# A two-block fp32 kernel on one core: a new order of loads, retention steps and weight rounding in its first segment

## The chip, the core and the metric

The kernel runs on one core of a Trainium2 chip. The metric is the device time of one execution in microseconds (us), as the median of several executions. Beside it stand single executions taken with the hardware profiler, whose span (first to last instruction) is about 1.8 us shorter than the time of the same execution. An execution is marked slow when it lies over 1.5% above the fastest of its kernel.

The engines are called by their short names where the profile does so: PE is the tensor engine's matmuls, DVE the vector engine, ACT the scalar engine, POOL GpSimd, SP the engine from which nearly all transfers are issued.

## The reference

A recurrent retention block, whose output feeds a SwiGLU feed-forward block, all in fp32 (batch 4, 8 heads, 768 positions, head size 64; model width 512, inner width 1536):

```python
for t in range(S):
    state = gamma * state + einsum('bhd,bhe->bhde', k[:, :, t], v[:, :, t])
    y[:, :, t] = scale * einsum('bhd,bhde->bhe', q[:, :, t], state)
x = y.transpose(0, 2, 1, 3).reshape(B * S, H * D)
g = x @ w_gate
out = (silu(g) * (x @ w_val)) @ w_out
```

## The kernel before

The kernel cuts the 3072 rows into four segments (`s` = 0 to 3) of six chunks of 128 rows. Retention of a chunk is three parts: `scores` (q times k, masked on DVE), `mix` (the output, copied by ACT into `xT`), `state` (update of the running state). All feed-forward products are done by a Strassen-like scheme with seven products for eight, so both factors need **sums**: S sums of the rows (`sums_x`), T sums of the weights (`sums_t`). The first segment goes through `up`, twelve units, one for each weight tile; as the weights come, they are rounded (three instructions on ACT, four on DVE, one addition on POOL: `convert_a`, `_b`, `_c`), summed and stored for the later segments, which use a second level of the scheme (`up2`). After each segment's up stage comes its down stage. The cuts of code below are shortened; `...` and comments stand for what is left out.

```python
def up(f):                       # one of 12 units of the first segment
    product(x, B11, a_up(0, 0)); copy(p1, x)
    if f: left[f - 1][0]()       # T4 product and both silus of the unit before
    sums_t(("up", f + 1, 0))     # DVE
    product(wb, T1, s1); copy(p5, wb)
    for p in at_block[f]: convert_b(p)          # DVE: half of a down tile, then the up tile
    for p in at_block[f][::-1]: convert_c(p)    # POOL: up tile, then the half
    product(x, T2, s2); copy(u2, x)
    product(wb, B22, s4)
    if f: left.pop(f - 1)[1]()   # DVE: both products with the gates
    tt(hT[:, f, 0], wb, u2, add)
    product(x, T3, s3); tt(hT[:, f, 1], x, p5, add)
    ...                          # convert_a of the next pieces (ACT), B21 product

# the start: all chunks loaded in order, a weight tile after chunks 2 and 4
retain(7); convert_a(u0); retain(3); convert_b(u0); convert_c(u0)
retain(3); sums_t(u0); retain(3); convert_a(u1); ...
for f in range(NF - 1): up(f)
...                              # T sums of the down tiles around the last up unit
```

In the first down stage, DVE also prepares the units of the second level between its other work: each is loaded from a store in DRAM, gets three sums, and is stored again. `step()` runs after every product (21 times).

```python
NU, RING = 21, 6                 # NU = 7 * NQ, NQ = 3
to_sum = list(range(RING - 1, NU, 2)) + list(range(RING - 2))   # 8 + 4 units
def step():
    k = count[0] = count[0] + 1
    retain((k > 2) + (4 < k < 13))            # retention of the next segment
    if count[1] * 20 < (k + 2) * len(to_sum): # one more unit's load
        load_unit(...); sums.extend(sums_u(n)); count[1] += 1
    while sums and count[2] * 20 < (k - 1) * 3 * len(to_sum):
        sums.pop(0)(); count[2] += 1          # the third sum also issues the store
```

## Time and profile before

| | before |
|---|---|
| median time | 743.3 us |
| span of the profiled run | 740.6 us |
| PE busy | 712.9 us (96%) |
| first product of S sums (T1 of unit 0) starts | 41.4 us |
| an up unit | 9.65 us |
| first down stage (end of the up stage to the next segment's second group of products) | 159.4 to 237.0 us |

### The profile page before, as it was taken

The numbers are of one execution on the slowest core, as the hardware profiler recorded it, in microseconds if no ns is written. First come the engines' busy times: TensorE is split into PE (matmuls) and PEld (weight loads), VectorE is DVE, ScalarE is ACT, GpSimd is POOL, SyncE is SP. The second block draws the span as 40 slices with busy tenths as digits, with TensorE's granted clock in tenths as the row PEclk, the third lists the DMA queues.
The fourth block names the chain that finished last, engine by engine and source line by source line (L and its number), as shares of the span: only waits on it lengthen the run. The fifth ranks groups of instructions, "written<-read, shape, count | busy, mean of one in ns | idle before, by whom it ended". The sixth has DMA issues, their size and how long they took to land.

```text
span 740.6 us, 11633 instructions
## 1 busy us (share of the span) xinstructions
PE 712.9 (96%) x4516; PEld 614.0 (83%) x4516; DVE 482.6 (65%) x829; ACT 241.8 (33%) x484; POOL 244.5 (33%) x152
## 2 busy tenths in 40 slices
PE   5789999999999999999999999999999999999997
PEld 5645555568888999997888999998888899999886
DVE  2899999997595787877454465758426356667420
ACT  2587777421211333321211324332121133233000
POOL 2533333423100547381210173454310053726000
PEclk9999999999999999999999999999999999999999
DMA  9968886458968667670643355660283055540010
GB/s 328 375 214 255 254 265 214 150 205 272 317 220 332 235 228 260 247 270 28 192 180 127 105 209 204 208 205 22 85 308 131 30 200 199 199 150 1 0 58 29
DMA packets 60823, 139.04 MB, mean 188 GB/s; under 512 B 4576, under 2 KB 27616, under 8 KB 60768
## 3 DMA queue, kind: packets, MB, share of 16 engines
q1 hardware_dynamic: 57312, 132.01, 52.2%
q10 hardware_dynamic: 3456, 6.29, 2.4%
q8 instruction: 35, 0.57, 0.3%
q14 instruction: 20, 0.16, 0.1%
HBM read 101.72 MB, written 36.57 MB: 187 GB/s over the span
## 4 chain that ended last, share of the span: by engine, by line
PE 82%; DVE 7%; issue 4%; POOL 2%; DMA 2%; ACT 2%; ACTq 0%; SPq 0%; DVEq 0%; POOLq 0%
PE bank L548 38%; PE bank L632 25%; PE bank L435 6%; PE bank L641 4%; PE bank L328 3%; PE bank L380 3%; PE bank L376 2%; POOL ring L265 2%; DVE ring L277 2%; PE bank L359 1%; DMA hT<-in_q_t_dram 1%; DMA hT<-in_k_t_dram 1%; DMA tab<-in_decays_dram 1%; DVE ring L252 1%; DVE xs L418 0%
## 5 line engine op out<-in xcount | busy, mean ns | idle before, releaser
L548 PE MATMUL bank<-loadp,ring 128*128 128x192 f32 x720 | 140.5, 327 | 2.8 <-ACT midp L513 2.8
L632 PE MATMUL bank<-wot,hsp 128*128 128x256 f32 x576 | 131.5, 383 | 0.0
L548 PEld LDWEIGHTS bank<-loadp,ring 128*128 128x128 f32 x720 | 120.5, 190 | 4.2 <-ACT midp L513 4.0
L632 PEld LDWEIGHTS bank<-wot,hsp 128*128 128x128 f32 x576 | 107.6, 190 | 16.3 <-issue 0.5
L513 DVE TENSOR_TENSOR iop<-bank,iop 128x384 f32<-128x384 f32 x144 | 79.7, 555 | 56.7 <-PE bank L548 53.6
L548 PE MATMUL bank<-xs,ring 128*128 128x192 f32 x432 | 87.8, 326 | 0.0
L513 POOL TENSOR_TENSOR iop<-hsp,midp 128x768 f32<-128x768 f32 x9 | 16.3, 1816 | 189.6 <-ACT hsp L513 149.4
L583 POOL TENSOR_TENSOR hT<-iop 128x768 f32<-128x768 f32 x36 | 66.5, 1848 | 35.8 <-DVE iop L513 35.8
L513 ACT COPY hsp<-bank 128x384 f32<-128x384 f32 x90 | 42.9, 479 | 99.5 <-PE bank L548 88.8
L548 PEld LDWEIGHTS bank<-xs,ring 128*128 128x128 f32 x432 | 73.1, 190 | 0.0
L435 PE MATMUL bank<-xs,ring 128*128 128x384 f32 x192 | 65.7, 497 | 2.8 <-DVE xs L418 2.8
L548 PE MATMUL bank<-xT,ring 128*128 128x192 f32 x324 | 66.2, 327 | 1.1 <-DVE iop L513 1.1
L632 PE MATMUL bank<-wot,hT 128*128 128x256 f32 x288 | 66.3, 383 | 0.0
L435 PEld LDWEIGHTS bank<-xs,ring 128*128 128x128 f32 x192 | 37.2, 194 | 29.5 <-DVE xs L418 3.4
L632 PEld LDWEIGHTS bank<-wot,hT 128*128 128x128 f32 x288 | 53.7, 190 | 8.5 <-issue 1.4
L548 PE MATMUL bank<-hsp,ring 128*128 128x192 f32 x288 | 56.8, 327 | 0.0
L513 DVE TENSOR_TENSOR midp<-bank,midp 128x384 f32<-128x384 f32 x72 | 40.0, 555 | 25.8 <-PE bank L548 24.3
L548 PEld LDWEIGHTS bank<-xT,ring 128*128 128x128 f32 x324 | 54.8, 190 | 2.3 <-DVE iop L513 2.2
L435 PE MATMUL bank<-xT,ring 128*128 128x384 f32 x144 | 51.0, 492 | 3.7 <-DVE hT L453 3.7
L548 PEld LDWEIGHTS bank<-hsp,ring 128*128 128x128 f32 x288 | 48.3, 190 | 0.5 <-ACT hsp L513 0.5
L435 PEld LDWEIGHTS bank<-xT,ring 128*128 128x128 f32 x144 | 26.5, 190 | 25.4 <-issue 9.0
L383 ACT COPY xT<-bank 128x512 f32<-128x512 f32 x24 | 14.1, 587 | 99.4 <-PE bank L380 96.6
(138 smaller groups left out, 983.4 us busy)
## 6 DMA issues: line engine op xcount, KB each, us to landing
ring<-unitt SPq DMA_DIRECT2D x50, 896.0 KB, 4.6
unitt<-ring SPq DMA_DIRECT2D x21, 896.0 KB, 4.6
unitb<-ring SPq DMA_DIRECT2D x12, 896.0 KB, 5.9
ring<-unitb SPq DMA_DIRECT2D x21, 512.0 KB, 5.7
out_dram<-iop ACTq DMA_DIRECT2D x24, 256.0 KB, 4.0
loadp<-in_w_val_dram SPq DMA_DIRECT2D x18, 256.0 KB, 5.8
loadp<-in_w_gate_dram SPq DMA_DIRECT2D x9, 512.0 KB, 6.4
midp<-in_w_out_dram SPq DMA_DIRECT2D x12, 256.0 KB, 3.1
```

The costliest lines, as they stand in the source:

```text
L265: nc.gpsimd.tensor_tensor(d.bitcast(I32), d.bitcast(I32), lo.bitcast(I32), op=ALU.add)
L277: sub(both, w[:, ds(B22, 2)], w[:, ds(B12, 2)], op=ALU.subtract)
L328: nc.tensor.matmul(sp[i][:, ts(n, P)], kt[r, n], qt[r, n], start=True, stop=True, skip_group_check=True)
L376: nc.tensor.matmul(y[r, ts(n, P)], prev[r, n], qd[r, n], start=(n == 0), stop=False, skip_group_check=True)
L380: nc.tensor.matmul(y[ds(D * i, D), ts(n, P)], vn[:, ts(2 * n + i, D)], a[i][:, n], start=(ci == 0 and n == 0), stop=True, skip_group_check ...
L383: nc.scalar.copy(xT[:, :, c // NCK % 2, ts(ci % L, P)], pairs(y))
L435: nc.tensor.matmul(o, w[:, slot, k], a[:, k], start=(start and k == 0), stop=(stop and k == KH - 1), skip_group_check=True)
L513: events.append((t, len(events), lambda: fn(*args, **kw)))
L548: nc.tensor.matmul(o[:, h], w[:, h, slot], rhs, start=(start and h == 0), stop=True, skip_group_check=True)
L583: by_block(9.5, 13.5, lambda r: pool(to[:, r], u2[:, r], p5[:, r], op=add))
L632: nc.tensor.matmul(o, a[:, k], wot[k][:, slot], start=(start and k == 0), stop=(k == FH - 1), skip_group_check=True)
L641: nc.tensor.matmul(o, a_dn(0, 0, u)[:, k], wot[k][:, B11], start=(k == 0), stop=(k == FH - 1), skip_group_check=True)
```

## The change

Its intent is to start the feed-forward products sooner. It replaces the loop of retention parts by a written order in which each letter is one part (s scores, m mix, t state, x S sums, a/b/c ACT's rounding, B/S DVE's, C POOL's, T T sums, U/D load of a tile), loads the last chunk ahead of the second weight tile, lets S sums read the retention output in PSUM, runs zero products at the very start, rounds the up tile ahead of the down half in each unit, moves the states of chunks 4 and 5 and the T sums of the down tiles into the first down unit, and starts the preparation of units later.

```diff
+    def sums_x(j): ...  # b(): the chunk's bank in PSUM instead of xT
-        tt(s1, a(1, 0), a(1, 1), op=ALU.add)
+        tt(s1, b(1, 0), a(1, 1), op=ALU.add)
...
+    do("""
+        s0 w6 s1 m0 m1 K0 t0 K1 s2 t1 g2 g3 Q2 s3 m2 x0 k2 q3 t2 s4 a0 b0 m3 k3 B0 t3 q4 c0
+        g4 s5 S0 g5 x1 m4 a1 q5 C0 U T0 b1 m5 x2 U D D
+    """)
...
+        beside[f, 1] = " ".join((each("BSC"), ...))     # up tile first
...
+            if s == 0:                                   # first down unit
+                sums_d(0); sum_h(1, 0)
+                second(0); do("t4")
+                sum_h(2, 0); sums_d(1)
+                second(1); do("t5")
+                sum_h(4, 0); sum_h(3, 0); sums_d(2)
...
-            retain((k > 2) + (4 < k < 13))
+            retain((k > 2) + (4 < k < 13) if s else (k > 5) + (7 < k < 18))
...
-            if count[1] < len(to_sum) and count[1] * 20 < (k + 2) * len(to_sum):
+            if count[1] < len(to_sum) and count[1] * 15 < (k - 5) * len(to_sum):
...
-            while sums and count[2] * 20 < (k - 1) * 3 * len(to_sum):
+            while sums and count[2] * 15 < (k - 6) * 3 * len(to_sum):
```

`second` is the B21 product, which used to stand between T3 and T4 of each row block; in the first two blocks of this stage T4 now follows T3 at once.

More of the change, by code (lines that the diff above doesn't have):

```diff
@@ L118, in places_of @@
         if n % 3 == 2:
-            return [ring[4 + i // 3][:, ts(i % 3, 512)] for i in range(4)]
+            return [ring[4 + i // 2][:, ts(i % 2, 512)] for i in range(4)]
         return [loadp[:, ts(4 * (n % 3) + i, 512)] for i in range(4)]
@@ L162, in load_unit, with sums_u @@
         units[n] = t
-    def sums_u(n):
+    def sums_u(n, engine=nc.vector):
         w = units[n]
-        sub = nc.vector.tensor_tensor
+        sub = engine.tensor_tensor
         def first():
@@ L207, in load_piece @@
             t = raw_places[kind].pop(0)
-            if kind == "down" or a > 1:
+            if kind == "down" or a:
                 raw_places[kind].append(t)
@@ L235, in words_of, with convert_a @@
         return d, r[:, :, 0], r[:, :, 1]
-    def convert_a(piece, *own):
+    def convert_a(piece, own, part=None):
         if piece in raw:
             d, lo, hi = words_of(piece)
-            nc.scalar.activation(d, hi.bitcast(F32), AF.Abs)
-            signs[piece] = []
-            for i, o in enumerate(own):
-                nc.scalar.copy(banks[o], hi[:, ts(i, 512)].bitcast(F32))
-                signs[piece].append(banks[o])
-            nc.scalar.activation(lo.bitcast(F32), lo, AF.Copy, scale=2.0 ** -51,
-                                 bias=2.0)
@@ L249, in convert_b @@
-    def convert_b(piece):
+            if part in (0, None):
+                nc.scalar.activation(d, hi.bitcast(F32), AF.Abs)
+            if part in (1, None):
+                signs[piece] = []
+                for i, o in enumerate(own):
+                    nc.scalar.copy(banks[o], hi[:, ts(i, 512)].bitcast(F32))
+                    signs[piece].append(banks[o])
+            if part in (2, None):
+                nc.scalar.activation(lo.bitcast(F32), lo, AF.Copy, scale=2.0 ** -51,
+                                     bias=2.0)
@@ new lines, in convert_b @@
+    def convert_b(piece, part=None):
+        if piece in raw:
+            d = words_of(piece)[0]
+            u = d.bitcast(U32)
+            if part in (0, None):
+                nc.vector.tensor_scalar(d, d, 122879.9921875, 2.0 ** -15, op0=ALU.min,
+                                        op1=ALU.max)
+                nc.vector.tensor_scalar(u, u, 3, None, op0=ALU.logical_shift_left)
+            if part in (1, None):
+                for i, t in enumerate(signs.pop(piece)):
+                    v = u[:, ts(i, 512)]
+                    nc.vector.scalar_tensor_tensor(v, t.bitcast(U32), 0x80000000, v,
+                                                   op0=ALU.bitwise_and,
+                                                   op1=ALU.bitwise_xor)
@@ L250, in convert_b, with convert_c @@
+    def convert_c(piece, halves=1):
         if piece in raw:
             d, lo, hi = words_of(piece)
-            nc.vector.tensor_scalar(d, d, 122879.9921875, 2.0 ** -15, op0=ALU.min,
-                                    op1=ALU.max)
-            u = d.bitcast(U32)
-            nc.vector.tensor_scalar(u, u, 3, None, op0=ALU.logical_shift_left)
-            for i, t in enumerate(signs.pop(piece)):
-                v = u[:, ts(i, 512)]
-                nc.vector.scalar_tensor_tensor(v, t.bitcast(U32), 0x80000000, v,
-                                               op0=ALU.bitwise_and,
-                                               op1=ALU.bitwise_xor)
@@ L262, in convert_c @@
-    def convert_c(piece):
-        if piece in raw:
-            d, lo, hi = words_of(piece)
-            nc.gpsimd.tensor_tensor(d.bitcast(I32), d.bitcast(I32), lo.bitcast(I32),
-                                    op=ALU.add)
+            n = d.shape[1] // halves
+            for i in reversed(range(halves)):
+                nc.gpsimd.tensor_tensor(d[:, ts(i, n)].bitcast(I32),
+                                        d[:, ts(i, n)].bitcast(I32),
+                                        lo[:, ts(i, n)].bitcast(I32), op=ALU.add)
@@ L267, in convert_c, with sums_t @@
             del raw[piece]
-        load_next(piece[0])
-    def sums_t(piece, engine=nc.vector):
+    def sums_t(piece, parts=range(3)):
         kind, a, h = piece
         w = span(piece)[0]
-        sub = engine.tensor_tensor
+        sub = nc.vector.tensor_tensor
         flat = w.rearrange("p a b -> p (a b)")
@@ L276, in sums_t @@
         both = flat[:, : 4 * n].rearrange("p (a b) -> p a b", b=2 * n)[:, :, :n]
-        sub(both, w[:, ds(B22, 2)], w[:, ds(B12, 2)], op=ALU.subtract)
-        sub(w[:, T2], w[:, B22], w[:, T1], op=ALU.subtract)
-        sub(w[:, T4], w[:, B21], w[:, T2], op=ALU.subtract)
+        for o, x, y in [((both, w[:, ds(B22, 2)], w[:, ds(B12, 2)])),
+                          ((w[:, T2], w[:, B22], w[:, T1])),
+                          ((w[:, T4], w[:, B21], w[:, T2]))][parts[0] : parts[-1] + 1]:
+            sub(o, x, y, op=ALU.subtract)
@@ L280, in sums_t, with scale @@
         if kind == "up":
             keep_wt(a)
-    at_block = [[("down", n // 2, n % 2) for n in range(2 * FH)
-                 if f == min(n, NF - 2)] +
-                [("up", f + 2, 0)] * (f + 2 < NF) for f in range(NF)]
+    pieces = [("up", f, 0) for f in range(NF)] + [
+        ("down", n % FH, 1 - n // FH) for n in range(2 * FH)]
+    sign_banks = {0: (0, 1), 1: (4, 5)}
+    def scale(what, engine):
+        return lambda n: what(cs[n], engine)
+    parts = {
+        "s": lambda n: scores(cs[n]), "m": lambda n: mix(cs[n]), "x": lambda n: sums_x(n),
+        "g": lambda n: decay(cs[n]), "t": lambda n: state(cs[n]), "w": lambda n: warm_up(n),
+        "k": lambda n: scale_k(cs[n]), "q": lambda n: scale_q(cs[n]),
+        "K": lambda n: scale_k(cs[n], nc.vector), "Q": lambda n: scale_q(cs[n], nc.vector),
+        "B": lambda n: convert_b(pieces[n], 0), "S": lambda n: convert_b(pieces[n], 1),
+        "C": lambda n: convert_c(pieces[n], 1 + (n == 0)), "T": lambda n: sums_t(pieces[n]),
+        "U": lambda n: load_next("up"), "D": lambda n: load_next("down"),
+        **{p: lambda n, i=i: convert_a(pieces[n], sign_banks.get(n, (6, 7)), i)
+           for i, p in enumerate("abc")}}
@@ new lines, in do @@
+    def do(order):
+        for o in order.split():
+            parts[o[0]](int(o[1:] or 0))
+    beside = {
+        (0, 0): "c1 B1 S1 C1 U D", (0, 2): "a2 b2", (0, 3): "c2", (0, 5): "T1",
+        (1, 0): "a3", (1, 1): "B2 S2 b3 B3 C2 U", (1, 2): "c3", (1, 4): "T2", (1, 5): "S3 C3 U",
+    }
+    halves = [[], [], [], [12], [13], [14], [15], [16], [17], [18], [19, 20, 21], [22, 23]]
+    sign_banks[3] = 4, 6
+    for f in range(2, NF):
+        new = list(range(f + 2, min(f + 3, NF))) + halves[f]
+        free = [6, 7, 4]
+        for n in new:
+            sign_banks[n] = [free.pop(0) for _ in range(2 if n < NF else 1)]
+        each = lambda ps: " ".join(f"{p}{n}" for p in ps for n in new)
+        beside[f, 0] = f"T{f + 1}" if f + 1 < NF else ""
+        beside[f, 4] = ""
+        beside[f, 1] = " ".join((each("BSC"), "U" * (f + 5 < NF), "D " * len(halves[f])))
+        beside[(f - 1, 4) if f > 2 else (2, 0)] += " " + " ".join(f"{p}{n}" for n in new for p in "abc")
@@ L287, in tile_retnet_swiglu, with aside @@
+    a, b = beside[2, 0][2:], beside[2, 1]
+    beside[2, 0], beside[2, 1], beside[2, 2], beside[2, 3] = "", "a4", "b4 c4", "T3 "+b
+    beside[11, 4] = "k4 k5"
+    beside[8, 2] = "D D"
+    def aside(f, place):
+        if (f, place) == (8, 2):
+            raw_places["down"][:0] = [hsp[:, ts(i, 1024)] for i in range(2)]
+        do(beside.get((f, place), ""))
     to_load = {"up": [("up", f, 0) for f in range(NF)],
-               "down": [("down", n // 2, n % 2) for n in range(2 * FH)]}
+               "down": [("down", n % FH, 1 - n // FH) for n in range(2 * FH)]}
@@ L291, in tile_retnet_swiglu @@
     raw_places = {"up": [loadp[:, ds(0, 2048)], loadp[:, ds(2048, 2048)],
-                         loadp[:, ds(0, 2048)], loadp[:, ds(2048, 2048)],
-                         hsp[:, ds(0, 2048)]],
+                         loadp[:, ds(0, 2048)], hsp[:, ds(0, 2048)]],
                   "down": [midp[:, ds(0, 1024)], midp[:, ds(1024, 1024)],
@@ L336, in scores, with scale_q, scale_k, decay @@
         att[c] = a
+    def scale_q(c, engine=nc.gpsimd):
+        if c % NCK:
+            qt = pairs(chunks[c][1])
+            engine.tensor_tensor(qt, qt, qdec, op=ALU.mult)
+    def scale_k(c, engine=nc.gpsimd):
         if c % NCK < NCK - 1:
             kd = chunks[c][3].rearrange("p (h d) -> p h d", h=H)
-            nc.gpsimd.tensor_tensor(
+            engine.tensor_tensor(
                 kd, kd, kdec[:, :, None].to_broadcast([P, H, D]), op=ALU.mult)
-        if c % NCK:
-            nc.gpsimd.tensor_tensor(qt, qt, qdec, op=ALU.mult)
+    def decay(c):
+        if 0 < c % NCK < NCK - 1:
+            for n in range(NP):
+                nc.scalar.activation(state_of(c)[:, n], state_of(c, 1)[:, n], AF.Copy,
+                                     scale=gdec[:, ds(n, 1)])
     def state(c):
@@ L349, in state @@
         vn, kd = chunks[c][2:]
-        new, old = state_of(c), state_of(c, 1)
-        if ci:
-            for n in range(NP):
-                nc.scalar.activation(new[:, n], old[:, n], AF.Copy,
-                                     scale=gdec[:, ds(n, 1)])
+        new = state_of(c)
         st = bank("st")[:, : NP * D].rearrange("p (n e) -> p n e", n=NP)
@@ L369, in mix @@
         a = att.pop(c)
-        y = bank("y")
+        y = banks[(0, 1, 2, 3, 7, 6)[first_chunks.index(c)]] if c in first_chunks else bank("y")
         if ci:
@@ L383, in mix, with first @@
         nc.scalar.copy(xT[:, :, c // NCK % 2, ts(ci % L, P)], pairs(y))
+        if c in first_chunks:
+            att[c] = pairs(y)
     def retention(s):
         cs = seg_chunks(s)
+        def first(n):
+            scores(cs[n])
+            scale_k(cs[n])
+            scale_q(cs[n])
         def last(n):
+            decay(cs[n])
             state(cs[n])
             del chunks[cs[n]]
-            if s and n + 3 < len(cs):
+            if n + 3 < len(cs):
                 load_chunk(cs[n + 3], places_of(n))
-        steps = [lambda: scores(cs[0])]
+        steps = [lambda: first(0)]
         for n, c in enumerate(cs):
             if n + 1 < len(cs):
-                steps.append(lambda n=n: scores(cs[n + 1]))
+                steps.append(lambda n=n: first(n + 1))
             steps.append(lambda c=c: mix(c))
@@ L414, in a, with b @@
             return xT[:, ds(KH * h, KH), i, ts(j, P)]
+        def b(i, h):
+            y = att.get(first_chunks[2 * j + i])
+            return a(i, h) if y is None else y[:, ds(KH * h, KH)]
         s1, s2, s3, s4 = (t[:, :, ts(j, P)] for t in xs)
         tt = nc.vector.tensor_tensor
-        tt(s1, a(1, 0), a(1, 1), op=ALU.add)
-        tt(s2, s1, a(0, 0), op=ALU.subtract)
-        tt(s4, a(0, 1), s2, op=ALU.subtract)
-        tt(s3, a(0, 0), a(1, 0), op=ALU.subtract)
+        tt(s1, b(1, 0), a(1, 1), op=ALU.add)
+        tt(s2, s1, b(0, 0), op=ALU.subtract)
+        tt(s4, b(0, 1), s2, op=ALU.subtract)
+        tt(s3, a(0, 0), b(1, 0), op=ALU.subtract)
     left = {}
@@ L458, in up @@
             left[f - 1][0]()
-        if f + 1 < NF:
-            sums_t(("up", f + 1, 0))
+        aside(f, 0)
         product(wb, T1, s1)
         nc.scalar.copy(p5, wb)
-        for p in at_block[f]:
-            convert_b(p)
-        for p in at_block[f][::-1]:
-            convert_c(p)
+        aside(f, 1)
         product(x, T2, s2, start=False)
         nc.scalar.copy(u2, x)
+        aside(f, 2)
         product(wb, B22, s4, start=False)
@@ L472, in up @@
         tt(hT[:, f, 0], wb, u2, op=add)
+        aside(f, 3)
         product(x, T3, s3, start=False)
         tt(hT[:, f, 1], x, p5, op=add)
-        for i, p in enumerate(at_block[f + 1] if f + 1 < NF else []):
-            convert_a(p, *((6, 7) if p[0] == "up" else ((4, 6)[i],)))
+        aside(f, 4)
         product(z, B21, a_up(0, 1))
         tt(c11, z, p1, op=add)
+        aside(f, 5)
         left[f] = gates, muls
@@ L627, in down @@
         x = banks[(u or 0) % 2][:, :DH]
-        cur = dict(hs)
         def product(o, slot, a, start=True):
@@ L646, in first, with second @@
                 step()
+        def second(u):
+            z = bank("wz")[:, :DH]
+            product(z, B21, a_dn(0, 1, u))
+            to = iop[:, ts(2 * (u % 2), DM)]
+            tt(to[:, :DH], z, first_dn.pop(u), op=ALU.add)
+            step()
         def more(*ns):
@@ L659, in down @@
             first(1)
-        elif u not in first_dn:
+            if s == 0:
+                sums_d(0)
+                sum_h(1, 0)
+                second(0)
+                do("t4")
+                sum_h(2, 0)
+                sums_d(1)
+                second(1)
+                do("t5")
+                sum_h(4, 0)
+                sum_h(3, 0)
+                sums_d(2)
+        elif u == 2:
             first(u)
-        p1 = first_dn.pop(u)
+        cur = dict(hs)
         wb = bank("wz")[:, :DH]
@@ L679, in down @@
         step()
-        z = bank("wz")[:, :DH]
-        product(z, B21, a_dn(0, 1, u))
-        tt(ev[0][:, :DH], z, p1, op=ALU.add)
-        step()
+        if s or u == 2:
+            second(u)
         product(x, T4, a_dn(1, 1, u), start=False)
@@ L690, in down, with warm_up @@
         step()
+    kept_vk = consts.tile([P, 2, 512], F32, name="kept_vk")
+    def warm_up(n):
+        for _ in range(n):
+            nc.tensor.matmul(banks[3][:, :P], warm[:, :P], warm[:, :P], start=True, stop=True,
+                             skip_group_check=True)
+    warm = consts.tile([P, P + 1], F32, name="warm")
+    nc.vector.memset(warm, 0.0)
+    nc.scalar.activation(warm[:, P:], warm[:, :1], AF.Silu)
+    warm_up(8)
     cs = seg_chunks(0)
@@ L697, in tile_retnet_swiglu @@
         hsp[:, ts(i, 512)] for i in range(6)]
-    load_chunk(cs[0], early[:2])
+    early[20:22] = early[18:20]
+    early[18:20] = [kept_vk[:, i] for i in range(2)]
+    early[22:] = [ring[i][:, ds(1024, 512)] for i in (4, 5)]
+    load_chunk(cs[0], early[0:2])
     nc.sync.dma_start(out=tab[:, :QDEC0], in_=decays[:, :QDEC0])
     load_chunk(cs[1], early[4:6])
-    load_chunk(cs[0], early[2:4])
+    load_chunk(cs[0], early[2:3])
+    load_chunk(cs[1], early[6:7])
     nc.sync.dma_start(out=tab[:, QDEC0:], in_=decays[:, QDEC0:])
-    load_chunk(cs[1], early[6:8])
-    for n in range(2, len(cs)):
-        load_chunk(cs[n], early[4 * n : 4 * n + 4])
-        if n in (2, 4):
-            load_next("up")
-    for _ in range(4):
-        load_next("down")
-    steps = retention(0)
+    load_chunk(cs[0], early[3:4])
+    load_chunk(cs[2], early[8:10])
+    load_chunk(cs[1], early[7:8])
+    load_chunk(cs[2], early[10:12])
+    load_chunk(cs[3], early[12:16])
+    load_chunk(cs[4], early[16:18])
+    load_next("up")
+    load_chunk(cs[4], early[18:19])
+    load_chunk(cs[5], early[20:23])
+    load_next("up")
+    load_chunk(cs[4], early[19:20])
+    load_chunk(cs[5], early[23:24])
+    do("""
+        s0 w6 s1 m0 m1 K0 t0 K1 s2 t1 g2 g3 Q2 s3 m2 x0 k2 q3 t2 s4 a0 b0 m3 k3 B0 t3 q4 c0
+        g4 s5 S0 g5 x1 m4 a1 q5 C0 U T0 b1 m5 x2 U D D
+    """)
     def retain(k):
@@ L715, in retain @@
                 steps.pop(0)()
-    u0, u1, u2 = (("up", f, 0) for f in range(3))
-    retain(7)
-    convert_a(u0, 0, 1)
-    retain(3)
-    convert_b(u0)
-    convert_c(u0)
-    retain(3)
-    sums_t(u0)
-    retain(3)
-    convert_a(u1, 2, 3)
-    retain(2)
-    convert_b(u1)
-    convert_c(u1)
-    retain(len(steps))
-    convert_a(("down", 0, 0), 4)
-    convert_a(u2, 6, 7)
     for f in range(NF - 1):
         up(f)
-    sums_t(("down", 0, 0), nc.gpsimd)
-    for j in (1, 2, 3):
-        sums_t(("down", j, 0))
     up(NF - 1)
-    sums_t(("down", 4, 0))
     down(0, None, None)(0, range(2))
@@ L743, in tile_retnet_swiglu, with sums_d @@
     muls()
-    sums_t(("down", 5, 0))
+    def sums_d(*parts):
+        for j in range(FH):
+            sums_t(("down", j, 0), parts)
     resident = list(range(RING - 2))
@@ L769, in tile_retnet_swiglu @@
             prepared = set(range(NU))
-        for n in (1, 2, 4, 3):
-            sum_h(n, 0)
+        if s:
+            for n in (1, 2, 4, 3):
+                sum_h(n, 0)
         steps = []
         if nxt:
+            att.clear()
             steps = retention(s + 1) + [lambda ps=ps: sums_2(*ps)
```

## The prediction

> **What bounds the kernel now.** I read the page first, then the engines' timelines of the first 60 us, then the waits of each stage. In the slices (40 of 18.5 us) the tensor engine is full except at the start:
>
> ```profile
> PE   5789999999999999999999999999999999999997
> DMA  9968886458968667670643355660283055540010
> ```
>
> Its busy time is 712.9 of 740.6 us, so 27.7 us is all that removing idle time can give, plus what it runs at a low clock. The timeline of the tensor engine shows where the first segment ends and the feed-forward part begins (start, duration; in brackets the idle time and who ended it):
>
> ```profile
> 27.44 1.16 PE L328 MATMUL bank<-hsp 64*128 64x128 f32 x16 [1.41 <-DMA hsp<-in_q_t_dram]
> ...
> 37.06 1.56 PE L435 MATMUL bank<-xT,ring 128*128 128x384 f32 x4
> 41.37 7.12 PE L435 MATMUL bank<-xs,ring 128*128 128x384 f32 x16 [2.75 <-DVE xs L418]
> 48.33 4.03 PE L435 MATMUL bank<-xT,ring 128*128 128x384 f32 x12
> 52.20 5.32 PE L435 MATMUL bank<-xs,ring 128*128 128x384 f32 x16
> ```
>
> The last chunk's queries land at 27.4, yet the first product of S sums (T1, line 435) starts only at 41.37, and its group takes 7.12 us instead of 5.32: the granted clock was 0.50 from 42 to 44 us (engines' busy time by stretches of 1 us). What held it is in the timelines of vector engine and GpSimd:
>
> ```profile
> 33.11 0.43 DVE L419 TENSOR_TENSOR xs<-xs,xT 128x256 f32<-128x256 f32 x1
> ...
> 38.75 2.56 DVE L418 TENSOR_TENSOR xs<-xT 128x256 f32<-128x256 f32 x1
> ```
> ```profile
> 38.64 2.39 POOL L265 TENSOR_TENSOR ring<-ring,loadp 128x1024 int32<-128x1024 int32 x1 [5.85 <-ACT state L353]
> ```
>
> The last S sum takes 2.56 us beside a GpSimd addition, and 0.43 alone. Before it stand a T sum (4.0 us, also beside GpSimd), a second S sum and the rounding of the second weight tile. So until 41 us the bound is an order of instructions on the vector engine, not the transfers.
>
> In the twelve up units, 9.65 us apart, the tensor engine waits once in each; in the whole run:
>
> ```profile
> PE bank L435 <- DVE hT L453: 3.7, 9, 0.7
> PE bank L548 <- ACT midp L513: 2.8, 4, 1.3
> ```
>
> A unit is 28 matmuls; 16 take 5.32 us, so it could run in 9.3. After 159 us nothing but these small waits is left: the first down stage (159 to 237 us) has a full tensor engine.
>
> **What the Trainium skill says.** (1) "TensorE: Matmul & The Clock Gate", Part 1: idle for about one 3.4 us window halves the clock, and sustained work restores it. The trace agrees: 16 score matmuls take 2.08 us at 4.3 us and 1.16 later, and the 2.75 us gap is followed by 0.50. (2) "SBUF — State Buffer", Who interferes with whom: a vector instruction with two SBUF inputs excludes a GpSimd one that reads SBUF; with at most one it does not. The trace agrees: 2.56 against 0.43 us above, while the mask products, with one PSUM input, keep 1.28 us for two beside a GpSimd addition at 25.2 us. (3) "DMA: Bandwidth & Descriptors", Anatomy of one DMA: a fixed cost of about 2 us, mostly the receipt of the last write. The trace's figure for the loads that matter below is larger, 5.3 us at the least, as they queue behind other transfers.
>
> **The start, part by part.** Landings of before fit 3.6 us + bytes / 365 GB/s (8.65 MB, the last queries, gives 27.3; seen 27.4). The new order puts the second weight tile (1 MB) behind them: after 7.34 MB, so 23.7 us; the first weight tile comes at 6.55 MB, 21.5 us. By the new order of each engine, with durations of before:
> - Rounding of tile 0: absolute value on ACT 21.5 to 22.6, clamp and shift 1.4 (alone; 2.7 beside GpSimd before) to 24.1, state add and last mask 0.4 + 1.3 behind the scores (23.8 to 24.9), so 26.2, signs 1.3 to 27.5, GpSimd in two halves 2 x 1.25 to 30.0.
> - Meanwhile S sums of the second pair, 4 x 0.43, to 29.2. They read PSUM, so GpSimd does not slow them. T sums with GpSimd idle, 1.55 (4.0 before), to 31.6. First of the last S sums, 0.43: 32.0. The tensor engine has finished the last mix at 28.9 and the B11 product (its half of the tile is rounded first) at 30.4.
>
> So T1 starts at about 32.1 instead of 41.4: **-9.3 us**. Its gap is 1.7 us, too short for the clock to fall: **-1.6 us** (7.12 - 5.32, a little held back). The zero matmuls at the start fill time spent waiting for the first transfer; they warm the clock for the first scores, which then wait for transfers anyway: 0.
>
> **Up units.** Before, a loop sets 9.65: GpSimd addition 2.4, T sum behind it (1.76 + 0.85, beside the second GpSimd addition), rounding of the down half 1.7, of the up tile 2.7, then GpSimd again. The change rounds the up tile first, so 0.69 of signs leaves the loop: about 9.0, below the 9.3 of the matmuls. The nine waits should go: **-3.6 us** with the edges. State updates of chunks 4 and 5 move into a stage where the tensor engine is full: two groups of 16 matmuls, 0.5 us each: **+1.0**. T sums of down tiles (6 x 1.55 = 9.3 us) move to the first down unit, spread behind 10 us of products that don't need them: 0.
>
> Sum so far: -9.3 - 1.6 - 3.6 + 1.0 = -13.5, so 729.8.
>
> **The first down stage: where I expect it to come back.** Between its products the vector engine prepares 16 units: load, three sums (0.68 + 0.43 + 0.43), store. Loads and stores share one queue, which waits in order:
>
> ```profile
> SPq L175 <- DVE ring L174: 34.1, 8, 11.8
> ```
> ```profile
> DMA to landing us min/median/max: 5.3/6.2/7.7
> ```
>
> The first line is the queue waiting for sums before a store (34.1 us in 8 waits), the second the landing of those loads. Counting the two conditions over the 21 steps: before, a unit is loaded in step 17 at the latest and summed two or three steps later. After, one unit is loaded in each of the steps 6 to 21, and from step 17 its sums stand **in the same step**. So the loads of units 12 to 15 each stand behind the store of the unit before, which waits for its sums: a serial ring of store issue 0.45, landing (5.3 seen behind a store; 4.7 assumed with the queue quiet), 1.55 sums, 0.1: 6.8 us a unit. The tensor engine's steps 17 to 21 last 2.7 us each, without retention between. The vector engine is also the one that reads T3's bank before T4 may add to it, and the first bank of the next stage.
> From the end of T2 in the last unit: last sums of unit 11 about 6 us later (S sums and second-level sums 4.0, unit 10's last and unit 11's 2.0), four rounds 27.2, second-level sums 2.8 and the first two reads 1.1: 37.1. The tensor engine can meanwhile do four products (10.8) and nine of the next stage (5.9): 16.7. The difference, **+20 us**, is idle. In steps 8 to 16 a load stands one step ahead, with steps of 4.5 us against 6.4: a few waits of 1 us, mostly hidden.
> 743.3 - 13.5 + 20 = 749.8; I put it at 748, as the ring's length is the least certain.
>
> **Rivals.** (a) The loads land early enough, or the tail is hidden: 729 to 732. For it: before, this stage had no such wait, and who moves these counts would look at a trace. Against it: the order of the queue. I give it 4 in 10. (b) The vector engine becomes the bound earlier in that stage, where T4 now follows T3 directly in the first two units: 4 to 8 us more, 754 to 758. Its busy share there was 66 of 90 us, for it only with waits. (c) The start stays bound by transfers, about 3 MB more by 30 us: second tile late. The tensor engine works on the first tile then; at most 2 us.
>
> **Range and chances.** The first mode gives 743 to 760, the second 727 to 733; the range spans both. Faster by 2% means below 728.5: only rival (a) with a start better than mine, 0.15. Slower means above 758.2: the ring and (b) together, 0.12. The rest is within.
>
> **What would show it.** First T1 product near 32 us with no clock below 1 after it; up units 9.3 us apart, without the tensor engine's waits for the vector engine; the first T sums 1.55 us together. In the first down stage, waits of the vector engine for unit loads, 4 to 5 us each, near its end, the tensor engine idle before T4 of the last unit and again early in the next stage, 15 to 28 us in all. If that stage shows no vector wait on a load, the ring is wrong and the time is near 730. If T1 starts later than 36 us, the start is wrong.

## More of the kernel before

One part of the page that the prediction does not show turned out to matter: the list of transfers (out<-in, issuer, how many, size each, us from issue to landing).

```profile
ring<-unitt SPq DMA_DIRECT2D x50, 896.0 KB, 4.6
unitt<-ring SPq DMA_DIRECT2D x21, 896.0 KB, 4.6
unitb<-ring SPq DMA_DIRECT2D x12, 896.0 KB, 5.9
ring<-unitb SPq DMA_DIRECT2D x21, 512.0 KB, 5.7
```

`unitt<-ring` is the store of a prepared unit, `ring<-unitb` its load: 21 in the whole run, as there are 21 units; 12 of them are prepared in the first down stage.

## The result

The changed kernel takes 733.4 us (median of 4, 732.9 to 733.9) against 743.3 us: 0.9868 of before, interval 0.9851 to 0.9885. A ratio here is the mean time of one kernel's fast runs over the mean of the other's in the same rounds, so not quite the ratio of the medians. A second set of runs gave 733.5 us and 0.9873. So it is 1.3% faster, clear of the noise, while the prediction had 748 us, slower than before.

The two traces, cut at the same three marks (starts of the same products):

| stretch | before, us | after, us | difference | predicted |
|---|---|---|---|---|
| start to T1 of unit 0 | 41.4 | 32.6 | -8.8 | -9.3 |
| up stage, to the second B11 product of the down stage | 118.0 | 113.9 | -4.1 | -5.2 (clock 1.6, units 3.6) |
| first down stage | 77.6 | 81.6 | +4.0 | +1.0 and +20 |
| the rest | 503.6 | 504.0 | +0.4 | 0 |
| span | 740.6 | 732.1 | -8.5 | |

In the timeline of PE after the change (line 513 is line 435 of before) the S product starts at 32.6 us, its 16 matmuls take 5.40 instead of 7.12 us, and an up unit lasts 86.72 - 77.69 = 9.03 us with no wait in it:

```profile
29.32 1.56 PE L513 MATMUL bank<-xT,ring 128*128 128x384 f32 x4
32.60 5.40 PE L513 MATMUL bank<-xs,ring 128*128 128x384 f32 x16 [1.72 <-DVE xs L496]
...
77.69 4.03 PE L513 MATMUL bank<-xT,ring 128*128 128x384 f32 x12
81.56 5.32 PE L513 MATMUL bank<-xs,ring 128*128 128x384 f32 x16
86.72 4.03 PE L513 MATMUL bank<-xT,ring 128*128 128x384 f32 x12
```

The waits of PE in the whole run (us in total, times, longest) show what was new: L772 is the reading of T3's bank, in the first down stage, and L550 and L534 stand in up units 1 to 3 (with one more of 0.2 us there they make 2.3).

```profile
PE bank L707 <- DVE iop L772: 2.5, 2, 1.8
PE bank L624 <- ACT midp L589: 2.5, 4, 1.3
...
PE bank L513 <- DVE hT L550: 1.6, 1, 1.6
...
PE bank L513 <- ACT iop L534: 0.5, 1, 0.5
```

And of DVE's waits, the one that the prediction had built on:

```profile
DVE ring L170 <- DMA ring<-unitb: 6.3, 4, 4.0
```

DVE waited for unit loads, but 6.3 us in four waits over two stages, not 4 to 5 us four times in a row at the end of the first down stage. The last wait in that stage was 0.74 us.

### The profile page after: what moved, and what is told of

Same layout as the page of the kernel before. It is cut to its first block, busy times and chain, and to the rows that moved or that the text cites. A ratio compares the mean times of both kernels' runs of the same rounds, so it can differ in the third digit from the quotient of the medians.

```text
span 732.1 us, 11713 instructions
## 1 busy us (share of the span) xinstructions
PE 713.2 (97%) x4544; PEld 615.4 (84%) x4544; DVE 469.3 (64%) x836; ACT 239.7 (33%) x484; POOL 237.4 (32%) x147
## 4 chain that ended last, share of the span: by engine, by line
PE 85%; DVE 5%; DMA 3%; issue 2%; ACT 1%; SPq 0%; ACTq 0%; DVEq 0%
PE bank L624 37%; PE bank L707 24%; PE bank L513 13%; PE bank L716 4%; PE bank L385 3%; PE bank L446 2%; PE bank L442 2%; DMA ring<-unitb 2%; DMA hsp<-in_w_gate_dram 1%; PE bank L424 1%; DVE ring L170 0%; DVE iop L589 0%; DVE ring L289 0%; DVE midp L391 0%; DVE ring L178 0%
## 5 line engine op out<-in xcount | busy, mean ns | idle before, releaser
L513 PEld LDWEIGHTS bank<-xs,ring 128*128 128x128 f32 x192 | 36.1, 190 | 29.2 <-issue 2.3
```

Of the source, the lines that this page charges most:

```text
L513: nc.tensor.matmul(o, w[:, slot, k], a[:, k], start=(start and k == 0), stop=(stop and k == KH - 1), skip_group_check=True)
```

## The experiments

Theory: the start and the up units behave as predicted; the first down stage does not, because the serial ring of load, sums and store that the prediction computed does not arise, as there are fewer units than it counted; what that stage lost (4.0 us) is, but for 0.3, the two moved state updates (two groups of 0.61 us) and two waits before T4 (2.5 us). Rivals: the ring is wrong as a mechanism (loads are quick or their waits hidden); the waits before T4 come from late loads; the gains of start and units have other causes than those named. All edits below are to the changed kernel.

### The ring, on purpose

```diff
-                sums.extend(sums_u(n))
+                for one in sums_u(n):
+                    one()
                 count[1] += 1
-            while sums and count[2] * 15 < (k - 6) * 3 * len(to_sum):
-                sums.pop(0)()
-                count[2] += 1
```

> The changed kernel, but in the first down stage each unit's load, three sums and store stand in one step, so each load stands behind the store of the unit before (what the prediction believed of the last steps, now for all 12 units). Ring theory: 0.45 issue + 5.3 landing + 1.55 sums = 7.3 us a unit, 12 units 88 us, against 66 us that the tensor engine has from step 6 to the end: vector engine waits for loads of 30 to 50 us in all, tensor engine idle 15 to 30 us in this stage, 748 to 764 us. Rival (a quiet queue lands loads in 3 us, or the waits are filled by other vector work): below 737 us.

Measured: 768.0 us (1.034 of before), 34.5 us over the changed kernel and 4 over the range of the ring theory. The first down stage took 115.7 us (146.1 to 261.8) instead of 81.6. DVE waited 46.0 us for loads in 11 waits. Its timeline, first sums of the sixth to the ninth of the twelve units (start, duration, idle before and releaser; other lines cut):

```profile
212.84 0.69 DVE L170 TENSOR_TENSOR ring<-ring 128x512 f32<-128x512 f32 x1 [4.15 <-DMA ring<-unitb]
...
220.38 0.69 DVE L170 TENSOR_TENSOR ring<-ring 128x512 f32<-128x512 f32 x1 [4.39 <-DMA ring<-unitb]
...
227.92 0.69 DVE L170 TENSOR_TENSOR ring<-ring 128x512 f32<-128x512 f32 x1 [2.08 <-DMA ring<-unitb]
...
235.52 0.69 DVE L170 TENSOR_TENSOR ring<-ring 128x512 f32<-128x512 f32 x1 [5.98 <-DMA ring<-unitb]
```

The units are 7.54, 7.54 and 7.60 us apart: the ring exists, and a round is even longer than the 6.8 us of the prediction (7.3 with the landing of 5.3 that the trace had shown). A load landed 5.5 us (median) after its issue, where the prediction had assumed 4.7. PE's longest waits stand where the prediction put them, before T4:

```profile
252.52 5.49 PE L707 MATMUL bank<-wot,hT 128*128 128x256 f32 x12 [10.66 <-DVE iop L772]
```

These 12 products take 5.49 us instead of 2.86, so part of the loss is a halved clock after the long waits (mean clock 0.978, against 1.000 of the changed kernel).

So the mechanism holds and its first rival falls. The changed kernel just does not enter it. With 12 units the conditions emit 0.8 loads a step, not 1.07, and the last unit is loaded in step 19 and summed in steps 20 and 21. The prediction's 16 units fit an NU of 28 (its own text names no NU), where the code and the list of 21 stores give 21 and 12. The very view of the kernel before from which it took the landings of 5.3 to 7.7 us counts the loads of the stage, of which the last belongs to the next segment:

```profile
L160 SPq DMA_DIRECT2D ring<-unitb x13: 359/379/454, 149.7 to 234.8; - x13
```

What the ring would have cost with 16 units, as predicted, was not run.

### Loads two steps earlier

```diff
-            if count[1] < len(to_sum) and count[1] * 15 < (k - 5) * len(to_sum):
+            if count[1] < len(to_sum) and count[1] * 15 < (k - 3) * len(to_sum):
```

> The changed kernel with unit loads two steps earlier, sums as they are. If the tensor engine's two waits before T4 (2.5 us) come from the vector engine waiting for loads (6.3 us in four waits): the waits for loads vanish and so do those before T4, 731 us. If they come from the order of the vector engine's work (sums of h and unit sums ahead of the reading of T3's bank): waits for loads vanish, those before T4 stay within 0.5 us, 733 us.

A miss for both theories: 740.1 us, 6.7 slower than the changed kernel. The waits before T4 stayed at 2.5 us, so they do not come from late loads. But waits for loads did not vanish; they moved behind the end of the stage, with one of 4.93 us, and PE then stood still early in the next segment:

```profile
236.74 1.65 PE L624 MATMUL bank<-xT,ring 128*128 128x192 f32 x4 [3.96 <-DVE midp L589]
238.18 1.48 PE L624 MATMUL bank<-loadp,ring 128*128 128x192 f32 x4
...
242.88 0.81 PE L624 MATMUL bank<-xs,ring 128*128 128x192 f32 x4
```

The groups of four after the gap take 1.48 us instead of 0.81: the granted clock was 0.50 from 236 to 242 us. The gap and the slow products behind it (20 in 6.1 us instead of 3.3) make 6.8 us, about the whole loss. Why the loads came late is in the waits of the issuing queue in this stage. Of this run:

```profile
SPq L160 <- DMA unitt<-ring: 34.2, 8, 7.3
SPq L175 <- DVE iop L772: 30.5, 1, 30.5
```

and of the changed kernel:

```profile
SPq L175 <- DVE iop L772: 36.3, 2, 31.5
SPq L175 <- DVE ring L174: 18.8, 9, 4.4
...
SPq L160 <- DMA unitt<-ring: 2.2, 2, 1.1
```

L160 issues loads, `unitt<-ring` is the landing of a store. Units take turns in four slots, so a load issued too early meets the store that is still emptying its slot. The queue then waits for that store to land (34.2 us instead of 2.2), and everything behind it waits too. The queue is closed into a ring from both sides: too little lead ties a load to the sums before it, too much ties it to the store four units back.

### Loads one step earlier

To test this reading, the load was moved by one step only, with T3's bank read first (the next experiment):

> T3's bank read first, and unit loads one step earlier. Slot theory (two steps earlier were bad because a load then waits in the queue for the store that empties its slot, 34 us of such waits): one step earlier leaves 1.75 steps between that store and the load, the queue's waits for stores stay under 8 us, time 730.5 to 731.5 us, as with T3's bank alone. Rival (any earlier load pushes the stores back): 733 us or more.

Measured: 731.6 us (731.2 to 734.0). DVE waited 1.4 us for loads, and the queue 5.0 us for stores:

```profile
SPq L160 <- DMA unitt<-ring: 5.0, 3, 2.3
```

Against 731.2 us for the early reading of T3's bank alone this is no gain. It supports the slots as the cause of the loss at two steps; a run with more slots, which would test it directly, was not made.

### T3's bank read first

```diff
-        more(1, 2, 4)
+        if s:
+            more(1, 2, 4)
         step()
         product(x, T3, cur[3], start=False)
         tt(ev[1][:, DH:], x, p5, op=ALU.add)
-        more(3)
+        more(*([3] if s else [1, 2, 4, 3]))
```

`more` are the sums of h for the next row block; three of them (1, 2, 4) move behind the reading, the fourth stood there before. In the changed kernel, DVE's timeline ahead of the first wait (PE stood from 171.6 to 173.4) is full of them, of a mask and of a unit's sums, all in front of the reading at 172.94:

```profile
165.70 0.95 DVE L695 TENSOR_TENSOR hsp<-hT 128x768 f32<-128x768 f32 x1
166.68 1.90 DVE L695 TENSOR_TENSOR hsp<-hsp,hT 128x768 f32<-128x768 f32 x1
168.62 1.68 DVE L695 TENSOR_TENSOR hsp<-hT,hsp 128x768 f32<-128x768 f32 x1
170.23 1.27 DVE L391 TENSOR_TENSOR midp<-bank,tab 128x512 f32<-128x512 f32 x2
171.43 0.68 DVE L170 TENSOR_TENSOR ring<-ring 128x512 f32<-128x512 f32 x1
172.14 0.42 DVE L178 TENSOR_TENSOR ring<-ring 128x256 f32<-128x256 f32 x1
172.59 0.42 DVE L174 TENSOR_TENSOR ring<-ring 128x256 f32<-128x256 f32 x1
172.94 0.42 DVE L772 TENSOR_TENSOR iop<-bank,iop 128x256 f32<-128x256 f32 x1
```

> The changed kernel with the four sums of h for the next row block moved behind the reading of T3's bank. Order theory: the waits before T4 (1.8 and 0.8 us) vanish, 730.5 to 731.5 us. Rival (vector engine simply lacks time in this stage): the wait turns up before T1 or T2 of the next block, 733 us.

Measured: 731.2 us (730.6 to 731.8), 0.9838 of before, interval 0.9823 to 0.9852. Both waits are gone and none takes their place; the stage takes 78.8 us (146.34 to 225.15). What is left over the 77.6 us of before is 1.2 us, and the two moved state groups take 0.61 each. So the 4.0 us of this stage are the order of DVE's work (2.8, of which 2.5 are the waits before T4) and the states (1.2). This version beats both kernels.

### All of it, with T sums moved back

This run joined the reading of T3's bank, loads two steps earlier and the T sums of three down tiles in the last up unit.

> The changed kernel with loads two steps earlier, T3's bank read first, and the T sums of three of the six down tiles moved back into the idle time of the vector engine in the last up unit. All theories of the first down stage together: no wait of the tensor engine before T4, first down stage 2.5 us shorter (79 instead of 81.6), 730 to 731 us. The 1.4 us of the two state updates stay, so it can't reach the 77.6 us of before.

Measured: 739.1 us. The waits before T4 are gone and the first down stage is 78.8 us, but the 3.3 us wait in the next segment is that of the loads experiment, and the T sums in the last up unit delay DVE's products with the gates (PE waits 1.2 us for them instead of 0.3). The stage is as long as with these T sums inside it (78.8 us), so they cost nothing there.

### The order of rounding in an up unit

```diff
-        beside[f, 1] = " ".join((each("BSC"), "U" * (f + 5 < NF), "D " * len(halves[f])))
+        beside[f, 1] = " ".join((" ".join(f"B{n} S{n}" for n in new[::-1]) + " " + each("C"), ...))
```

> The changed kernel with one thing put back: in an up unit the half of the down tile is rounded ahead of the up tile on the vector engine, as before. Loop theory (GpSimd addition, T sum, roundings follow each other in a ring that was longer than the matmuls): units 3 to 10 go back from 9.03 to 9.4 to 9.7 us, 3 to 5 us in all, 736 to 738 us. Rival (units got shorter because the vector engine has less to do): stays at 733 us.

Measured: 739.0 us, 0.9941 of before. PE's timeline is that of before again:

```profile
99.66 2.82 PE L513 MATMUL bank<-xT,ring 128*128 128x384 f32 x8 [0.34 <-DVE hT L531]
102.32 5.32 PE L513 MATMUL bank<-xs,ring 128*128 128x384 f32 x16
107.48 1.45 PE L513 MATMUL bank<-xT,ring 128*128 128x384 f32 x4
109.26 2.82 PE L513 MATMUL bank<-xT,ring 128*128 128x384 f32 x8 [0.33 <-DVE hT L531]
```

A unit is 9.60 us with one wait of 0.33 in it, although DVE runs the same 836 instructions as in the changed kernel. So the ring POOL addition, T sum, rounding, POOL addition sets the unit. The order of two roundings alone is worth 5.5 us, or 5.0 against the 733.9 us of the run without zero products on the same chip (below): half of the change's 9.9 or a little more. In the traces the up stage takes 119.0 us instead of 113.9.

### S sums from SBUF

```diff
-            return a(i, h) if y is None else y[:, ds(KH * h, KH)]
+            return a(i, h)
```

> The changed kernel with the S sums reading SBUF only. Port theory: the second pair's sums (27.7 to 29.4 us) meet the GpSimd additions (27.9 to 30.5 us) and end about 2 us later, first T1 product at 34 to 35 instead of 32.6 us; [...]the clock may fall too (another 1.5 us): 734.5 to 737 us. Rival: no change, 733 us.

Measured: 735.9 us (734.2 to 736.8), beside 733.9 for the run without zero products on the same chip. The sums of the second pair do collide (0.42 each in the changed kernel):

```profile
28.12 1.42 DVE L497 TENSOR_TENSOR xs<-xs,xT 128x256 f32<-128x256 f32 x1
29.57 1.40 DVE L498 TENSOR_TENSOR xs<-xT,xs 128x256 f32<-128x256 f32 x1
```

This is the case of "SBUF — State Buffer", Who interferes with whom: two SBUF inputs on DVE against a POOL instruction that reads SBUF. One SBUF input alone did not make a DVE instruction safe, though: in the kernel before, the clamp and the shift of tile 0 (20.85 to 23.6 us) have one each, and took 1.04 and 1.65 us beside POOL, 0.69 each alone. The sums end 2.0 us later, but 1.2 us of that DVE would have spent waiting for POOL anyway. The gap before T1 grew from 1.72 to 2.45 us. The profiled run kept its clock at 1.00; the other three executions have mean clocks of 0.997 to 0.998 and are the slower ones (735.7 to 736.8). So the loss on the path is 0.75 us, and half clock in most executions fits the rest; that was not seen in a trace. The expectation of T1 at 34 to 35 us was too high.

### No zero products

```diff
-        for _ in range(n):
+        for _ in range(0):
```

> The changed kernel without the zero products. Prediction's step: they fill time spent waiting for transfers, so 0: scores of the first two chunks at half clock (2.1 us each instead of 1.2 to 1.7), first T1 product at 32.6 as it is, 733 us. Rival: the clock comes up late enough to delay the chain, T1 at 33.5 to 35 us, 734 to 736 us.

Measured: 733.9 us (733.3 to 734.7), against 733.4 and 733.5: no effect that these runs resolve. Scores of the first two chunks took 2.08 us each as expected (half speed by their duration; the record of the granted clock shows 1.00 there), and T1 started at 33.3 us. That is within the scatter: in the runs here whose start is unchanged up to T1 it lies between 32.3 and 34.2.

### Second weight tile ahead of the last chunk

```diff
-    load_chunk(cs[5], early[20:23])
     load_next("up")
+    load_chunk(cs[5], early[20:23])
```

> The changed kernel with the second weight tile (1 MB) loaded ahead of the last chunk again, as before. Transfer theory: last queries land 2.8 us later (26.6 instead of 23.9), scores, mask and signs follow, first T1 product about 2.5 us later, 35 us: 735 to 737 us. Rival (order of the vector engine alone was what mattered): within 0.5 us of the changed kernel.

Measured: 737.4 us. T1 started at 36.1 us, 2.8 later than in the run beside it on the same chip:

```profile
27.43 1.43 PE L385 MATMUL bank<-hsp 64*128 64x128 f32 x16 [4.17 <-DMA hsp<-in_q_t_dram]
28.79 1.97 PE L442 MATMUL bank<-hT,state 64*64 64x128 f32 x16
```

The transfer theory holds, with the size foreseen. The wait for the queries also halves the clock for a while (1.97 instead of 1.09 us), which the kernel before, with queries as late, did not suffer. So up to a third of the 8.8 us of the start is the order of loads, and 0.75 us are the inputs of the S sums, by the run above. The rest, some 5 us, is put down to the order of work on DVE and POOL by the timelines; no run puts that order back alone.

### The waits of up units 1 to 3

```diff
-        g4 s5 S0 g5 x1 m4 a1 q5 C0 U T0 b1 m5 x2 U D D
+        g4 s5 S0 g5 x1 m4 a1 q5 C0 U m5 U T0 b1 x2 D D
...
-    ... beside[2, 3] = "", "a4", "b4 c4", "T3 "+b
+    ... beside[2, 3] = "", "a4", "b4 c4", "T3"
+    beside[2, 4] = b + beside[2, 4]
```

with T3's bank read first. The edit also moves the last mix (`m5`) forward. The changed kernel itself ran beside it:

> The changed kernel itself again, as the measure for the two runs beside it: 733.4 us, 0.987 of before.

> T3's bank read first, and in up units 0 to 3: the fourth tile's load issued ahead of the store of the first T sums, and the rounding of tile 4 moved behind the reading of T3's bank in unit 2. If the 2.3 us of waits of the tensor engine in units 1 to 3 come from these two orders, they go: 729 to 729.5 us. Rival (the vector engine has no time to spare there, so the wait moves to the products of gate and value or to the next T sum): 730.5 to 731.5 us, as with T3's bank alone (731.2).

Measured: 733.2 us (731.7 to 734.4), beside 733.5 for the changed kernel. A miss: the waits for DVE became one for ACT, longer than the sum of the old ones.

```profile
66.20 5.83 PE L514 MATMUL bank<-xs,ring 128*128 128x384 f32 x12 [2.71 <-ACT iop L535]
```

The 12 products behind this gap take 5.83 us instead of 4.14: the granted clock was 0.50 from 68 to 70 us. The two executions with a mean clock of 1.000 took 731.7 and 732.5 us, the two with 0.998 took 734.0 and 734.4, so the halved clock is part of the loss against 731.2. The rival is right in kind: this shift only moved the wait. Whether another order would save those 2.3 us is open.

## Why the prediction was wrong

- **Start, -9.3:** right; T1 at 32.6 for 32.1, by the order of engines that the prediction wrote down, each step within 0.7 us of its time. The share of the load order was shown by putting the load back (2.8 us).
- **Clock, -1.6:** right; the granted clock stayed at 1.00 after the 1.7 us gap. Its statement that the trace agrees with the skill's window of 3.4 us was too smooth: the gap that it shows, 2.75 us, is shorter.
- **Zero products, 0:** right within the scatter.
- **Up units, -3.6:** the ring and its cure were right, as the run with the old order shows. The size was off in both directions: a unit is 9.03, not 9.3 us, because a group of 16 matmuls starts 5.16 us before the next group, while its row in the timeline, 5.32 us, overlaps that group; and units 1 to 3 got waits of 2.3 us that the prediction did not look for. Clock and units together gave -4.1 for -5.2; that it came so near is partly luck, as these two errors nearly cancel.
- **States, +1.0, and T sums of the down tiles, 0:** right; 1.2 and 0, as the stage is 78.8 us with all these sums in it or with half of them moved back.
- **The ring in the first down stage, +20: this step failed.** In its words, "Between its products the vector engine prepares 16 units", "one unit is loaded in each of the steps 6 to 21, and from step 17 its sums stand in the same step". There are 12 units. The mis-sized term is a count read from the code, not a duration: with 12, loads stay ahead of sums and no such ring forms. In place of 20 us of idle time the stage lost 4.0, and the last wait of DVE for a load in it was 0.74 us. The ring made on purpose ran at 7.5 us a unit for 6.8 and cost 34.5 us over twelve units, so the mechanism had been sound and its length 10% short. The count could have been checked on the profile of before, with 21 stores and 13 loads in the view that the prediction read. This one step turned a forecast of about 730 us into 748.
- **Rival (a)**, 729 to 732 us at 4 in 10, is the mode that came, 1.4 us above its range. "The loads land early enough" is what happened; the reason, that there are fewer of them, was not among its grounds.
- **Rival (b)**, DVE late with T3's bank now that T4 follows T3 at once, was put at 4 to 8 us on top of the ring. It occurred without the ring, with 2.5 us, and reading that bank first removed it.
- With the failed step left out, the prediction's own sum is 729.8 us, 3.6 below the measured 733.4. The two traces differ by 8.5 us for its 13.5 (the execution profiled was among the fastest of before and the slowest of after): 0.5 us of this miss lie in the start, 1.1 in the up stage, 3.0 in the first down stage, 0.4 behind it.

## What to carry to other kernels

Before you compute what a schedule does, check the counts that you read from the code against the counts of the profile (here 21 stores): an exact mechanism with a wrong count gave a forecast with the wrong sign. When a transfer queue waits in order, a prefetch has a lower and an upper limit; don't let the load queue behind the work before it, nor behind the slot's own store. In a pipeline of several engines, put first on the shared engine what the other engine needs next: moving one rounding forward was worth about 5 us, moving three sums back 2.2 us.

## What the Trainium skill lacked or had wrong

- "TensorE: Matmul & The Clock Gate", Part 1, tells to avoid idle gaps over about 3.4 us. Here shorter gaps were enough at times: after one of 2.75 us in the kernel before the clock was 0.50 (42 to 44 us), and after one of 2.71 us in the run on up units 1 to 3 as well (68 to 70 us). But gaps of 1.72 us ahead of T1 and one of 2.45 us left it at 1.00, and so did gaps of 2.71 and 2.84 us in the starts of the repeated changed kernel and of the run with T sums moved back: 16 score products took 1.16 us behind them, as at full speed. So among these gaps of 2.45 to 2.84 us the length alone does not decide.
- "DMA: Bandwidth & Descriptors", Issuing engines are not separate DMA queues, says that several issuing engines save only the time to initiate. No page tells what a wait inside one issuing queue costs the transfers behind it: with loads two steps earlier the queue stood 34.2 us for landings of stores (2.2 us in the changed kernel), and the run was 6.7 us slower.
